# Issuing the first five loads of pass two from ScalarE's queue instead of SyncE's

## The chip, the cores and the metric

One core of a Trainium2 chip runs the whole kernel. The metric is the device time of one execution in microseconds.

## The reference

The reference scales an image of 384 x 384 pixels and 384 channels (bf16, 113 MB) by a factor for each channel, which it gets from the mean of the whole image:

```python
g = jnp.einsum("bhwc->bc", x) / (H * W)
gp = jnp.pad(g, ((0, 0), (pad, pad)))            # k = 1, so pad = 0
s = jnp.zeros_like(g)
for i in range(k):
    s = s + gp[:, i:i + C] * w1d[i]
s = _sigmoid(s)
return x * s[:, None, None, :]
```

No pixel can be scaled before the last one has been summed. So every kernel has two passes over the image, and what the on-chip memory cannot hold has to be read twice.

## The kernel before

Pass one loads all rows (a "row" is 384 channels on each of 128 partitions, 98,304 bytes in all) and sums them on TensorE. It keeps as many rows as it can in one big on-chip tile, `arena`: 71 raw, and 296 more in groups in which VectorE has folded four rows' bits into the space of three. The other 785 rows, the streamed ones, are loaded again in pass two. Pass two scales what is kept, stores it, and loads streamed rows into the places that come free.

All instructions go through a small scheduler. It takes them in program order, finds what each has to wait for from the rows that it reads and writes, and gives each transfer a semaphore of its own queue (a counter that is raised as the transfer lands, and that others can wait for):

```python
        if dma:
            q = self.queued.setdefault(eng, [])
            s.lane = (eng, len(q) % self.LANES)
            ...
            q.append(s)
    ...
                waits = [(sem(d), d.rank * (16 if d.dma else 1)) for d in s.waits]
                ...
                for h, v in waits:
                    eng.wait_ge(h, v)
                ins = s.emit()
```

An engine's queue works in order: while it waits for the semaphore of one transfer, it issues nothing behind that. (The trace before shows it. The stores that the first load of pass two needs had landed by 273.31 us. But the load stood behind a store that was issued at 274.27 us, and was itself issued at 274.70 us.) Loads and stores share one such queue, SyncE's:

```python
    def load(chunk, a, lo, hi):
        r0, n = chunk
        fl.add(
            "SP",
            lambda: nc.sync.dma_start(out=arena[:, a : a + hi - lo, :], in_=view(xf, r0, n)[:, lo:hi, :]),
            writes=rows(a, hi - lo), dma=True,
        )
    ...
    def store(chunk, a, lo, hi):
        r0, n = chunk
        return fl.add(
            "SP",
            lambda: nc.sync.dma_start(out=view(of, r0, n)[:, lo:hi, :], in_=arena[:, a : a + hi - lo, :]),
            reads=rows(a, hi - lo), dma=True,
        )
```

The order of all work of pass two is fixed when the kernel is built, by a loop that imitates the passing of time. It decides when VectorE scales rows (`scale`), when it unfolds a group, when a store is sent, and when enough places are free for the next load:

```python
        if landed and (ahead < PENDING or not can):
            chunk, a, lo, n, end = landed.popleft()
            scale(a, n)
        ...
        if got and todo < N_STREAM:
            n, a = max(got)
            n = min(n, CAP, N_STREAM - todo)
            ahead = backlog()
            if n >= BIG or n == N_STREAM - todo or (ahead < LOW and n >= 8) or ahead < LAST:
                load(STREAMED, a, todo, todo + n)
                ...
```

A load waits until the stores of the rows that it overwrites have landed. A store waits until VectorE has scaled its rows.

## Time and profile before

| | before |
|---|---|
| time, median of 6 runs | 721.47 us (720.91 to 722.41) |
| profiled span | 720.1 us |
| bytes moved | 303.8 MB, about 430 GB/s wherever the DMA is full |
| VectorE busy, whole span | 69% |
| VectorE busy, 269 to 310 us | 38.66 of 41 us |
| last load of pass one lands, first store issued | 267.5 us, 270.06 us |
| last store lands | 718.0 us |

The DMA here is the core's 16 DMA engines, which move data between the main memory and the on-chip memory. The page's slices (a digit is the busy share of a fortieth of the span, in tenths) tell when the DMA engines are full. The table by stretches gives the same for any window, with the GB/s moved. The issues and waits of SyncE's queue tell what each load and store waited for. The lines of each are in the prediction below.

### The profile page before, as it was taken

To read this page: it belongs to the slowest core of one execution; us is meant where nothing else is said; L and a number is where in the kernel's file an instruction comes from. 1 tells how busy PE (TensorE), PEld (TensorE's weight loads), DVE (VectorE), ACT (ScalarE), POOL (GpSimd) and SP (SyncE) were. 2 spreads that over 40 slices of the span, in tenths; PEclk is the share of its full clock that TensorE was granted. 3 is DMA by queue.
4 is the path that set the end of the run, shared out by engine and by line. 5 is a ranking of instruction groups with operands and counts; after the bars stand their busy time and mean duration, and the time that the engine had idled before them with its cause. 6 is when DMAs were issued, how large, how long until landed. Compare 5 with 4: busy or idle time off the path is not lost.

```text
span 720.1 us, 2041 instructions
## 1 busy us (share of the span) xinstructions
PE 213.6 (30%) x1202; PEld 0.3 (0%) x3; DVE 496.4 (69%) x470; ACT 115.4 (16%) x92; POOL 0.2 (0%) x4
## 2 busy tenths in 40 slices
PE   4678778897987770000000000000000000000000
PEld 0000000000000000000000000000000000000000
DVE  4600004788999719989899999999996991558500
ACT  3600003566777510002000000000000000000000
POOL 0000000000000000000000000000000000000000
PEclk9798999999999995555555555555555555555555
DMA  9999999999999979999999999999999999999996
GB/s 382 431 439 428 426 431 430 435 436 430 423 427 428 427 321 355 427 431 424 414 429 433 430 433 433 434 431 432 439 430 440 428 435 436 433 431 434 433 435 299
DMA packets 18877, 303.79 MB, mean 422 GB/s; under 512 B 2098, under 2 KB 2098, under 8 KB 4658
## 3 DMA queue, kind: packets, MB, share of 16 engines
q1 hardware_dynamic: 18864, 303.67, 98.7%
q8 instruction: 4, 0.07, 0.0%
q14 instruction: 7, 0.06, 0.0%
q10 hardware_dynamic: 2, 0.00, 0.0%
HBM read 190.41 MB, written 113.25 MB: 422 GB/s over the span
## 4 chain that ended last, share of the span: by engine, by line
DMA 60%; DVE 27%; PE 4%; ACT 2%; SPq 0%; issue 0%; DVEq 0%; another core or an unknown queue 0%
DMA arena<-in_x_dram 43%; DVE arena L451 19%; DMA out_dram<-arena 17%; DVE arena L275 5%; PE bank L242 4%; DVE arena L281 3%; ACT arena L312 2%; SPq L235 0%; ACT s_bf L442 0%; DVEq L112 0%; SPq L772 0%; SPq L112 0%; SPq L106 0%
## 5 line engine op out<-in xcount | busy, mean ns | idle before, releaser
L451 DVE TENSOR_TENSOR arena<-arena,s_bf 128x1536 bf16<-128x1536 bf16 (+8 forms) x103 | 242.2, 2390 | 57.8 <-DMA arena<-in_x_dram 41.9
L275 DVE TENSOR_SCALAR arena<-arena 128x1536 uint16<-128x1536 uint16 (+2 forms) x247 | 145.5, 634 | 114.9 <-DMA arena<-in_x_dram 102.2
L242 PE MATMUL bank<-arena,ones 128*128 128x384 bf16 x1151 | 205.2, 340 | 46.1 <-DMA arena<-in_x_dram 45.9
L312 ACT ACTIVATE arena<-arena 128x3072 uint16<-128x3072 uint16 (+1 forms) x38 | 102.5, 2696 | 142.4 <-DVE arena L275 142.4
L281 DVE TENSOR_TENSOR arena<-arena 128x1536 uint16<-128x1536 uint16 (+2 forms) x114 | 121.1, 1062 | 5.2 <-PE bank L242 2.7
L524 PE MATMUL bank<-odd,ones 128*128 128x1 bf16 x1 | 0.2, 184 | 329.2 <-DVE odd L519 329.2
L385 ACT COPY arena<-bank 128x512 uint32<-128x512 uint32 (+1 forms) x7 | 4.0, 571 | 61.9 <-DMA out_dram<-arena 61.8
L242 PE MATMUL bank<-zeros,ones 128*128 128x384 bf16 x48 | 8.3, 326 | 0.0
L312 ACT ACTIVATION_READ_ACCUMULATOR arena<-arena 128x1 f32 x38 | 7.1, 186 | 0.0
L385 ACT COPY bank<-arena 128x512 uint32<-128x512 uint32 (+1 forms) x7 | 3.6, 567 | 0.0
L442 ACT ACTIVATE s_bf<-bank,w_sc 128x384 bf16<-128x384 f32 x1 | 0.6, 582 | 14.5 <-PE bank L242 14.5
L255 PE MATMUL bank<-arena,ones 128*128 128x384 bf16 x1 | 0.5, 476 | 6.8 <-DMA arena<-in_x_dram 6.8
L745 ACT ACT_TABLE_LOAD x1 | 1.3, 1283 | 0.7 <-PEq L761 0.7
L342 DVE TENSOR_SCALAR w_sc<-bank 128x1 f32<-128x1 f32 x1 | 0.2, 159 | 1.1 <-PE bank L337 1.1
L332 DVE MEMSET ones<- 128x128 bf16 x1 | 0.2, 165 | 1.0 <-SPq L106 1.0
L337 PE MATMUL bank<-w_bf,ones 1*128 1x1 bf16 x1 | 0.2, 182 | 2.1 <-DMA w_bf<-in_w1d_dram 2.1
L524 PEld LDWEIGHTS bank<-odd,ones 128*128 128x128 bf16 x1 | 0.1, 103 | 588.4 <-DVE odd L519 588.4
L528 DVE CAST odd_i<-bank 128x1 int32<-128x1 f32 x1 | 0.2, 157 | 0.3 <-PE bank L524 0.3
L514 DVE TENSOR_REDUCE worst<-seen 128x1 f32<-128x38 f32 x1 | 0.2, 184 | 0.0
L519 DVE TENSOR_SCALAR odd<-worst 128x1 bf16<-128x1 f32 x1 | 0.2, 156 | 0.0
L333 DVE MEMSET zeros<- 128x64 uint32 x1 | 0.1, 112 | 0.0
L255 PEld LDWEIGHTS bank<-arena,ones 128*128 128x128 bf16 x1 | 0.1, 104 | 6.8 <-issue 6.8
(5 smaller groups left out, 0.5 us busy)
## 6 DMA issues: line engine op xcount, KB each, us to landing
arena<-in_x_dram SPq DMA_DIRECT2D x15, 4608.0 KB, 33.3
arena<-in_x_dram SPq DMA_DIRECT2D x22, 1248.0 KB, 11.3
out_dram<-arena SPq DMA_DIRECT2D x8, 3072.0 KB, 30.3
arena<-in_x_dram SPq DMA_DIRECT2D x6, 3072.0 KB, 27.4
out_dram<-arena SPq DMA_DIRECT2D x12, 1248.0 KB, 11.9
out_dram<-arena SPq DMA_DIRECT2D x3, 4608.0 KB, 39.8
arena<-in_x_dram SPq DMA_DIRECT2D x3, 4512.0 KB, 37.9
out_dram<-arena SPq DMA_DIRECT2D x3, 4512.0 KB, 27.7
```

Of the source, the lines that this page charges most:

```text
L242: return pe.add_instruction(mybir.InstMatmult(name=nc.get_next_instruction_name(), ins=[pe.lower_ap(rhs), pe.lower_ap(ones[:])], outs=[pe. ...
L255: return nc.tensor.matmul(acc, lhsT=ones[:], rhs=arena[:, i, :], start=first, stop=last)
L275: lambda: nc.vector.tensor_scalar(out=dst, in0=src, scalar1=s0, scalar2=s1, op0=op0, op1=op1),
L281: "DVE", lambda: nc.vector.tensor_tensor(out=dst, in0=a, in1=b, op=op), reads=reads, writes=writes
L312: lambda: nc.scalar.activation(out=y, in_=y, func=ACTF.Copy, accum_out=seen[:, 2 * k + i : 2 * k + i + 1]),
L332: fl.add("DVE", lambda: nc.vector.memset(ones[:], 1.0), writes=["ones"])
L337: lambda: nc.tensor.matmul(votes, lhsT=ones[0:1, :], rhs=w_bf[0:1, 0:1], start=True, stop=True),
L385: "ACT", lambda: nc.scalar.copy(dst.bitcast(u32), src.bitcast(u32)), reads=reads, writes=writes
L442: lambda: nc.scalar.activation(out=s_bf[:], in_=acc, func=ACTF.Sigmoid, scale=w_sc[:, 0:1]),
L451: lambda: nc.vector.tensor_tensor(out=v, in0=v, in1=s_bf[:, None, :].to_broadcast([P, n, C]), op=Op.mult),
L524: lambda: nc.tensor.matmul(votes, lhsT=ones[:], rhs=odd[:], start=True, stop=True),
L745: nc.scalar.preload_act_table(ACTF.Sigmoid)
```

## The change

The intent: while a load on SyncE's queue waits for a landed store, stores behind it that are ready can't be issued. So the first five loads of pass two move to the queue of ScalarE, which has nothing else to do then.

```diff
-    def load(chunk, a, lo, hi):
+    def load(chunk, a, lo, hi, queue="SP"):

         r0, n = chunk
+        start = nc.sync.dma_start if queue == "SP" else nc.scalar.dma_start
         fl.add(
-            "SP",
-            lambda: nc.sync.dma_start(out=arena[:, a : a + hi - lo, :], in_=view(xf, r0, n)[:, lo:hi, :]),
+            queue,
+            lambda: start(out=arena[:, a : a + hi - lo, :], in_=view(xf, r0, n)[:, lo:hi, :]),
             writes=rows(a, hi - lo), dma=True,
         )
...
+    n_loads, N_ASIDE = 0, 5
...
-                load(STREAMED, a, todo, todo + n)
+                load(STREAMED, a, todo, todo + n, "ACT" if n_loads < N_ASIDE else "SP")
+                n_loads += 1
```

## The prediction

> **What bounds the kernel now.** I read the page from the top. Its slices of DMA share and of moved bytes come first, because the kernel moves much more than it computes.
>
> ```profile
> span 720.1 us, 2041 instructions
> PE 213.6 (30%) x1202; PEld 0.3 (0%) x3; DVE 496.4 (69%) x470; ACT 115.4 (16%) x92; POOL 0.2 (0%) x4
> DMA  9999999999999979999999999999999999999996
> GB/s 382 431 439 428 426 431 430 435 436 430 423 427 428 427 321 355 427 431 424 414 429 433 430 433 433 434 431 432 439 430 440 428 435 436 433 431 434 433 435 299
> HBM read 190.41 MB, written 113.25 MB: 422 GB/s over the span
> ```
>
> The reader is to see that the 16 DMA engines are at nine tenths or more in 38 of 40 slices, at about 430 GB/s, while the busiest compute engine, VectorE, has 69%. 303.7 MB at 430 GB/s are 706 us; the other 14 us are the start, the gap between the passes, and the end. Pass two (scale by the sigmoid and store) begins near 269 us. The input has 113.25 MB, the same as what is written, so pass two reads again 190.41 - 113.25 = 77.2 MB and moves 77.2 + 113.2 = 190.4 MB: 443 us at 430 GB/s. Its first packets flow at 271 us and its last at 718 us, 447 us. So about 4 us in all stand between pass two and a full DMA.
>
> Where those are I asked of the table by stretches (columns: length, busy of the engines, clock, DMA share, GB/s).
>
> ```profile
> 268.00:270.00 2.00, 0.43 (x3) 0.00 (x0) 0.92 (x2) 0.58 (x1) 0.00 (x0) 1.00 0.00 0
> 270.00:272.00 2.00, 0.00 (x0) 0.00 (x0) 2.00 (x3) 0.00 (x0) 0.00 (x0) 1.00 0.56 227
> ...
> 276.00:278.00 2.00, 0.00 (x0) 0.00 (x0) 2.00 (x1) 0.00 (x0) 0.00 (x0) 0.50 0.98 270
> 278.00:280.00 2.00, 0.00 (x0) 0.00 (x0) 2.00 (x2) 0.00 (x0) 0.00 (x0) 0.50 0.91 258
> ```
>
> ```profile
> 271.00:281.00 10.00, 0.00 (x0) 0.00 (x0) 10.00 (x5) 0.00 (x0) 0.00 (x0) 0.55 0.93 332
> 281.00:345.00 64.00, 0.00 (x0) 0.00 (x0) 61.60 (x54) 4.00 (x7) 0.00 (x0) 0.50 1.01 427
> 345.00:350.00 5.00, 0.00 (x0) 0.00 (x0) 4.93 (x8) 0.00 (x0) 0.00 (x0) 0.50 1.00 392
> 350.00:718.00 368.00, 0.18 (x1) 0.10 (x1) 279.38 (x211) 0.00 (x0) 0.00 (x0) 0.50 1.00 429
> ```
>
> From 281 us on the DMA is full. The loss is 10 x (430 - 332)/430 = 2.3 us in 271 to 281, some 0.4 us in 345 to 350, and the rest at the end, where the packets thin out from 714 to 718 us because some DMA engines finish 3.6 us after others. Note 276 to 280: the engines are busy, yet move 264 GB/s. In the packet records, 6144-byte packets that elsewhere take 234 ns take 330 to 390 ns on average there, and one 2.1 us. That is slowness of packets, not lack of work.
>
> Then the queue of SyncE, which the change is about: its waits between 268 and 310 us (total us, times, longest), and its issues in order of time (start, length; each landing time named below is that of the transfer's last semaphore update in the trace).
>
> ```profile
> SPq L461 <- DVE arena L451: 37.4, 12, 14.4
> SPq L235 <- DMA out_dram<-arena: 7.8, 4, 3.0
> ```
>
> ```profile
> 270.06 4.54 SPq L461 DMA_DIRECT2D out_dram<-arena  x4
> 274.70 0.40 SPq L235 DMA_DIRECT2D arena<-in_x_dram  x1
> 275.94 10.00 SPq L461 DMA_DIRECT2D out_dram<-arena  x5
> 287.50 6.65 SPq L235 DMA_DIRECT2D arena<-in_x_dram  x3
> 294.20 0.43 SPq L461 DMA_DIRECT2D out_dram<-arena  x1
> 295.31 0.33 SPq L235 DMA_DIRECT2D arena<-in_x_dram  x1
> 301.82 9.59 SPq L461 DMA_DIRECT2D out_dram<-arena  x4
> ```
>
> The five loads concerned are the one at 274.70, the three of 287.50 to 294.15 and the one at 295.31. Stores wait almost only for VectorE (37.4 us, 12 times); loads wait for the landing of the store that frees their rows (7.8 us, 4 times, the longest 3.0).
>
> **What the Trainium skill says.** "DMA: Bandwidth & Descriptors", section "Issuing engines are not separate DMA queues": DMAs started by ScalarE and by SyncE run on the same 16 DMA engines and interleave; starting them on several engines saves only sequencer time. The trace before can't show two queues at work (its one transfer on the other queue has a few bytes), but that one queue alone holds 427 to 434 GB/s agrees that nothing is left to add. The same page, "Queues, rings and completion order": each DMA engine goes round-robin between the rings that have work, packet by packet, and the two issuing engines own one ring each. So a load on the second ring no longer stands behind the stores queued before it: it takes about half the bandwidth at once. No run so far shows this. Its "Rules for kernel authors" says that spreading DMAs over queues doesn't help bandwidth; I rest the main estimate on that.
>
> **The change part by part.** No work is added or removed: 8 + 13 + 13 + 13 + 8 = 55 rows of 98,304 bytes, 5.4 MB or 12.6 us of DMA time, change the ring. The order on VectorE and the order of stores stay. An issue takes 0.33 to 0.40 us of a sequencer; five come to 1.8 us, moved from SyncE, which here mostly waits, to ScalarE, which between the sigmoid's end (269.05) and the bank copies (330.80) does nothing.
>
> Step 1, stores that no longer wait behind a load. Issued after load 1 is the store at 275.94, which waited for VectorE anyway: 0 us. After loads 2 to 4 comes the store at 294.20; its rows were ready when VectorE ended at 293.84: 0.36 us. After load 5 comes the store at 301.82, again waiting for VectorE: 0. Sum 0.4 us of earlier issue, for a store that then lands at 306.98, 12.8 us after issue. With 12 us of work queued ahead, issuing it 0.4 us earlier ends nothing earlier: worth 0.
>
> Step 2, loads that no longer wait behind a store. Load 1 needs the first two stores, landed at 272.37 and 273.31, and stood behind the fourth store, issued at 274.27 after VectorE. It can go at about 273.35, 1.35 us sooner. Loads 2 to 5 were issued at 287.50, 290.48, 293.83 and 295.31, and the stores they need landed at 287.48, 290.46, 293.81 and 295.29: they go 0.02 us after what frees their rows, so the queue held them by nothing.
>
> Step 3, does load 1 fill the hole? From issue to first packet the first store took 0.86 us (270.06 to 270.92). Load 1's packets then begin near 274.2. The hole in the packets is 272.9 to 273.45, and the third store's packets fill from there; at 274 to 276 the DMA is already at 412 GB/s. So at most the idle parts of 277 to 280 (busy 0.93, 0.87, 0.93, together 0.27 us) are filled by 0.8 MB offered sooner. Gain 0 to 0.3 us.
>
> Step 4, sharing. Load 2 landed at 298.25, as four stores' remains were ahead. With half the bandwidth from about 288.3 its 1.28 MB (2.97 us alone) land after about 6 us, near 295. The stores it passes land later by up to the same 3 us, so loads 3 to 5 are issued 1.5 to 3 us later, yet land earlier too, near 298 to 304 instead of 301.20, 304.17 and 309.27. VectorE's one wait for a load in this stretch, 2.2 us before 309.30, goes. VectorE is then some 2 us ahead; but what it feeds is a DMA with 7 to 12 us of work queued, so the end doesn't move.
>
> Sum: 0 (step 1) - 0.15 (steps 2 and 3) + 0 (step 4): 721.45 - 0.15, about 721.2.
>
> **The rivals.** First, the hole is due to the queue's order, as the change supposes: then up to 2.3 us of 271 to 281 come back and the time is 719.2. For it speaks that the low rate begins with the first load. Against it: engines busy at 0.91 to 0.98, slow packets. A variant is that the second ring lets an engine move a store's packet while a load's is held up, which would save part of the 1.5 us of the slow packets: near 720.
>
> Second, sharing hurts: the stores passed by loads land up to 3 us later, loads that wait for those stores are issued later, and if the DMA ran dry there it would be lost: up to +3 us, 724.5. Against it: the bytes queued at any time are the same or more as long as the loads are issued, and before had a queue of 7 us at its shortest here (last load landed at 309.27, next store issued at 301.82). Alternating reads and writes packet by packet might also cost efficiency; 5% of the about 25 us in which 5.4 MB of loads and as much of stores share would be 1.3 us: 722.5.
>
> Third, VectorE were the limit: its 2.2 us of idle time would be saved, 719.2. Against it: the DMA's full slices up to 718 us.
>
> Fourth, the slow packets of 276 to 280 and 343 to 348, which leave some DMA engines up to 3.6 us behind at the end, fall otherwise: 1 to 2 us either way.
>
> **Range and chances.** The middle is 721.0, a little under the sum for the first rival, which is likelier than the second. The first and third rival bring 719, the second and fourth 723; 8 times in 10 it should lie from 718.6 to 723.2. Two per cent are 14.4 us, more than all that pass two loses to anything but moving its bytes (4 us), so faster by that is 1%; slower needs a stall that the queue of 7 us or more would have to swallow first: 1%; within, 98%.
>
> **What would show each step.** Step 1: no store of 270 to 302 issued over 0.5 us earlier for the queue's sake. Step 2: load 1 issued by ScalarE near 273.4, loads 2 to 5 within 0.1 us of a store's landing. Step 3: 271 to 281 still at 320 to 360 GB/s; near 420 there means that the first rival is right. Step 4: load 2 lands near 295, 6 to 8 us after issue instead of 10.75, the stores beside it up to 3 us later, and VectorE's wait at 309 shrinks; rate from 281 on still 425 to 430. Below 415 over 285 to 310 means that sharing costs. The prediction is wrong if the DMA shows slices below 9 tenths after 281 us, or if a rate over 436 GB/s shows that two rings carry more than one.

## More of the kernel before

The kernel before and a kernel compared with it always ran on the same chip and in the same rounds.

## The result, and the profile after

The changed kernel takes 721.87 us (median of 6 runs, 721.08 to 722.42), against 721.47 us before. The ratio is 1.0003, with a 95% interval of 0.999 to 1.0016. A ratio here is the mean time of one kernel's fast runs over that of the other's fast runs in the same rounds, so it is not quite the ratio of the medians. The time is the same.

The page of the changed kernel, its span, its DMA slices, and its queues (packets, MB, share of 16 engines):

```profile
span 719.3 us, 2044 instructions
DMA  9999999999999979999999999999999999999997
GB/s 383 426 444 431 426 428 435 436 436 427 424 426 426 428 327 349 427 432 425 422 425 437 429 439 428 430 435 430 438 423 440 429 435 435 432 432 437 430 435 320
q1 hardware_dynamic: 18144, 298.26, 96.9%
q10 hardware_dynamic: 722, 5.41, 2.0%
```

The change is in effect: 5.41 MB, the five loads, moved to queue q10. The slices look as before: 14 and 15, in which pass two begins, have 327 and 349 GB/s after 321 and 355. (The profiled span is 0.8 us shorter. The medians of all runs don't show that as a gain.)

ScalarE's issues in the changed kernel, one line for each of the five loads (start, length):

```profile
273.21 0.36 ACTq L236 DMA_DIRECT2D arena<-in_x_dram  x1
286.17 0.33 ACTq L236 DMA_DIRECT2D arena<-in_x_dram  x1
289.16 0.33 ACTq L236 DMA_DIRECT2D arena<-in_x_dram  x1
294.36 0.33 ACTq L236 DMA_DIRECT2D arena<-in_x_dram  x1
299.15 0.33 ACTq L236 DMA_DIRECT2D arena<-in_x_dram  x1
```

And what SyncE's queue waited for in the changed kernel between 268 and 310 us:

```profile
SPq L462 <- DVE arena L452: 49.0, 13, 14.4
```

The waits of loads are gone from SyncE: all that is left there is stores that wait for VectorE. That was the intent, and it worked. But the loads themselves gained little. The stores that loads 2 to 5 need landed at 286.15, 289.14, 294.34 and 299.13 us, each 0.02 us before the issue of the load. Taking a load out of the queue does not land the store that it waits for.

The stretches of pass two in the changed kernel (length, busy time of the engines, clock, DMA share, GB/s):

```profile
271.00:281.00 10.00, 0.00 (x0) 0.00 (x0) 10.00 (x5) 0.00 (x0) 0.00 (x0) 0.63 0.95 326
...
285.00:310.00 25.00, 0.00 (x0) 0.00 (x0) 22.00 (x21) 0.00 (x0) 0.00 (x0) 0.50 1.01 429
281.00:345.00 64.00, 0.00 (x0) 0.00 (x0) 59.98 (x53) 3.99 (x7) 0.00 (x0) 0.50 1.01 428
345.00:350.00 5.00, 0.00 (x0) 0.00 (x0) 4.96 (x7) 0.00 (x0) 0.00 (x0) 0.50 1.01 414
350.00:718.00 368.00, 0.19 (x1) 0.11 (x1) 280.60 (x213) 0.00 (x0) 0.00 (x0) 0.50 1.00 428
```

The slow start of 271 to 281 us is still there, at 326 GB/s after 332. In the packet records it has only moved along with the first load, from 276 to 280 us to 275 to 278.5 us. While loads and stores share the engines on two rings (285 to 310 us), the DMA moves 429 GB/s, against 426 before. In this stretch sharing costs no efficiency and brings none.

What did change is the order in which things land:

| load | issue before / after | lands before / after |
|---|---|---|
| 1 (8 rows) | 274.70 / 273.21 | 282.59 / 279.73 |
| 2 (13 rows) | 287.50 / 286.17 | 298.25 / 295.65 |
| 3 (13 rows) | 290.48 / 289.16 | 301.20 / 300.94 |
| 4 (13 rows) | 293.83 / 294.36 | 304.17 / 306.03 |
| 5 (8 rows) | 295.31 / 299.15 | 309.27 / 310.86 |

Loads 2 and 3 are issued 1.3 us earlier, but not for the queue's sake. The stores that they need start to finish no earlier than before (for load 2, the first of the 16 engines is done at 285.56 us, after 285.32 before); the engines are only less spread (0.6 us from the first to the last, after 2.2).

Loads 2 and 3 overtake stores, which then land later. The eight-row store issued at about 285.5 us, for example, lands at 299.13 us instead of 295.29. Load 5 needs that store, so it is issued 3.8 us later and lands 1.6 us later. VectorE's wait for loads between 298 and 320 us (total, times, longest), before and then after:

```profile
DVE arena L451 <- DMA arena<-in_x_dram: 2.2, 1, 2.2
```

```profile
DVE arena L452 <- DMA arena<-in_x_dram: 3.8, 2, 2.1
```

It grew by 1.6 us instead of vanishing, and the end did not move. So there are three things to test. Is it the throughput of the DMA that sets the end? How much delay does the queued work swallow? And is it sharing that made loads 4 and 5 late?

### The profile page after: what moved, and what is told of

The parts are those of the page before. It is cut to its first block, busy times and chain, and to the rows that moved or that the text cites. A ratio compares the mean times of both kernels' runs of the same rounds, so it can differ in the third digit from the quotient of the medians.

```text
span 719.3 us, 2044 instructions
## 1 busy us (share of the span) xinstructions
PE 213.0 (30%) x1202; PEld 0.3 (0%) x3; DVE 495.9 (69%) x470; ACT 115.4 (16%) x92; POOL 0.2 (0%) x4
## 3 DMA queue, kind: packets, MB, share of 16 engines
q10 hardware_dynamic: 722, 5.41, 2.0%
## 4 chain that ended last, share of the span: by engine, by line
DMA 52%; DVE 31%; ACT 5%; PE 5%; another core or an unknown queue 1%; issue 0%; SPq 0%; DVEq 0%
DMA arena<-in_x_dram 36%; DVE arena L452 20%; DMA out_dram<-arena 16%; DVE arena L276 7%; ACT arena L313 5%; PE bank L243 5%; DVE arena L282 4%; SPq L236 0%; ACT s_bf L443 0%; DVEq L112 0%; SPq L776 0%; SPq L106 0%
## 6 DMA issues: line engine op xcount, KB each, us to landing
arena<-in_x_dram SPq DMA_DIRECT2D x15, 4608.0 KB, 33.9
```

## The experiments

My theory is the prediction's: the DMA's throughput sets the end, and the queue of issued work hides what happens before it. The rivals are that the order in SyncE's queue costs time, that VectorE sets the end, and that two rings do harm because loads overtake stores.

**All loads of pass two aside.** The changed kernel with one number changed:

```diff
-    n_loads, N_ASIDE = 0, 5
+    n_loads, N_ASIDE = 0, 1000
```

> The changed kernel, but every load of pass two goes through ScalarE's queue, none through SyncE's. My theory (the DMA engines' throughput sets the end; 7 us or more are always queued): same time, 721.5 us +- 1.5, rate 425 to 434 GB/s after 281 us, though SyncE's waits for landed stores (126 us in the changed kernel) all leave its queue. Rival (order in the queue costs, but five loads were too few to show it): faster by 3 us or more. Second rival (two rings share, stores land later and loads that wait for them come later): slower by 2 us or more, with VectorE waiting longer for loads than the 4.6 us of 268 to 420 us in the changed kernel.

Measured: 727.56 us against 721.87 us, ratio 1.008 (1.0066 to 1.0094). My theory is wrong here, and the second rival holds: more of the change is slower, clearly. VectorE's waits for loads between 268 and 420 us are 8.8 us, after 4.6 in the changed kernel. The stretches where it loses:

```profile
380.00:386.00 6.00, 0.00 (x0) 0.00 (x0) 6.00 (x4) 0.00 (x0) 0.00 (x0) 0.50 1.02 336
448.00:454.00 6.00, 0.00 (x0) 0.00 (x0) 5.93 (x12) 0.00 (x0) 0.00 (x0) 0.50 1.01 369
584.00:588.00 4.00, 0.00 (x0) 0.00 (x0) 4.00 (x3) 0.00 (x0) 0.00 (x0) 0.50 0.57 209
596.00:600.00 4.00, 0.00 (x0) 0.00 (x0) 4.00 (x2) 0.00 (x0) 0.00 (x0) 0.50 0.85 301
```

The kernel before moves 434, 442, 430 and 433 GB/s in the same stretches. In the third line the DMA runs dry (share 0.57) while VectorE is busy all the time. In the first two it is busy throughout (1.02 and 1.01) and slow nevertheless. The last two runs below take this apart.

**A late load left out.** The kernel before without one load of 44 rows.

```diff
-                load(STREAMED, a, todo, todo + n)
+                if n != 44:
+                    load(STREAMED, a, todo, todo + n)
```

> The kernel before without its load of 44 rows near 608 us (wrong result on purpose: those rows keep old data). It takes 44 x 98,304 bytes = 4.33 MB out of the DMA, 10.0 us at 432 GB/s. My theory (throughput of the DMA sets the end): faster by 9 to 10.5 us, 711 to 712.5. Rival (VectorE or the order of issues sets the end): faster by under 3 us.

Measured: 711.40 us against 721.87, ratio 0.9865 (0.985 to 0.988); the result is wrong. The gain is 10.5 us by the medians and 9.7 us by the ratio, for bytes worth 10.0 us, and the DMA stays full where the load was missing:

```profile
600.00:640.00 40.00, 0.00 (x0) 0.00 (x0) 14.04 (x5) 0.00 (x0) 0.00 (x0) 0.50 1.00 430
```

Late in pass two the bytes set the end, one for one.

**VectorE delayed by three passes, and by nine.** The kernel before, with passes over the rows of the second load that leave them as they are (3 or 9 for `K`).

```diff
                 chunk, a, lo, n, end = landed.popleft()
+                if chunk == STREAMED and lo == 8:
+                    for _ in range(K):
+                        bits(flat(a, n), flat(a, n), XOR, 0, AND, 0xFFFF, rows(a, n), rows(a, n))
```

> The kernel before with three more passes of VectorE over the 13 rows of the second load of pass two, near 299 us, that change no value: about 3 x 1.5 = 4.4 us of delay for VectorE and for every store after it. My theory (the store issued at 301.82 finds 7.5 us of queued work, as the last load lands at 309.27): time unchanged within 0.7 us. Rival (VectorE or the wait of stores for it sets the end): slower by 2.2 (4.4 less its own idle 2.2) to 4.4 us.

> As the one with three, but nine passes, about 13 us of delay. My theory: the 7.5 us queued, less about 1 us from issue to first packet, are used up, and the DMA runs dry for 13 - 6.5 = 6 us: slower by 4 to 8 us, with a hole in the GB/s near 309 to 316 us and none in the run with three passes. Rival (VectorE sets the end): slower by 11 to 13 us. Rival (something other than DMA and VectorE): under 2 us.

Measured: with three, 723.56 us, ratio 1.0023 (1.0007 to 1.0038), about 1.7 us slower; with nine, 732.53 us, ratio 1.0149 (1.0134 to 1.0165), 10.7 us slower. Both are more than I expected. The nine passes come nearer to the rival's 11 to 13 us than to my 4 to 8, and the 1.7 us of the three passes lie between my 0.7 and its 2.2. The DMA with three passes (4.44 us of work), then with nine (13.42 us):

```profile
305.00:309.00 4.00, 0.00 (x0) 0.00 (x0) 4.00 (x3) 0.00 (x0) 0.00 (x0) 0.50 0.88 369
```

```profile
306.00:316.00 10.00, 0.00 (x0) 0.00 (x0) 9.83 (x7) 0.00 (x0) 0.00 (x0) 0.50 0.08 35
```

With nine, the dry stretch loses 10 x (430 - 35)/430 = 9.2 us. So the queued work swallowed 13.4 - 9.2 = 4.2 us of delay, not the 6.5 that I had worked out (7.5 less 1 from issue to first packet). I had counted to the landing of the last load, 309.27 us. But that load's first update came at 306.66 us: the DMA engines are spread over 2.6 us, and 14 of the 16 were done with it by 307.29 us. The other 1.5 us of the loss are a slow stretch after the dry one (394 GB/s in 316 to 336 us, 20 x 36/430 = 1.7 us). With three passes the DMA runs dry too, where I expected no hole: that costs 0.6 us, and a slow stretch after it (396 GB/s in 309 to 330 us) another 1.7 us.

So the theory "it is all swallowed" is right for small delays only. If VectorE is delayed early in pass two, the first 4 us or so are hidden and what goes beyond them comes through nearly in full, with some 1.5 us for a slow stretch on top.

**The five loads left out.** The kernel before, the first five loads of pass two not issued; in a second run, told below, only the first one not issued. Their outputs are wrong, which doesn't matter for the times.

```diff
+    n_loads, N_SKIP = 0, 5       # 0, 1 in the next run
...
-                load(STREAMED, a, todo, todo + n)
+                if n_loads >= N_SKIP:
+                    load(STREAMED, a, todo, todo + n)
+                n_loads += 1
```

> The kernel before without the five loads concerned (wrong result on purpose). They are 5.41 MB, 12.6 us of DMA time. My theory: not all of it is gained, because early in pass two VectorE only just feeds the DMA: the queue that lasts to 309.3 us would end at 296.7, while the next store needs VectorE until 301.8: some 5 to 6 us of hole near 297 to 303, and a gain of 5.5 to 9 us. Rival that the change rested on (stores wait behind these loads, and that costs the time): the stores go out sooner and the whole 12.6 us or more are gained. Rival that the loads are free: under 2 us.

Measured: 719.52 us against 721.22, ratio 0.9974 (0.9958 to 0.9989). Bytes worth 12.6 us are gone, and the time falls by 1.7 us. This is less than I expected, and within what I had given for the rival that these loads are free. Two stretches of the DMA, and one of the whole early part, in which the third busy number is VectorE's:

```profile
289.00:294.00 5.00, 0.00 (x0) 0.00 (x0) 5.00 (x4) 0.00 (x0) 0.00 (x0) 0.50 0.17 69
...
297.00:302.00 5.00, 0.00 (x0) 0.00 (x0) 4.97 (x5) 0.00 (x0) 0.00 (x0) 0.50 0.00 0
...
269.00:310.00 41.00, 0.00 (x0) 0.00 (x0) 40.90 (x32) 0.00 (x0) 0.00 (x0) 0.52 0.71 300
```

I had found one dry stretch and missed the other. Together they lose 9.2 us of DMA time, and a slow stretch after them (345 GB/s in 312 to 321 us) another 1.8: that is why so little of the 12.6 us is gained. VectorE is busy for 40.90 of 41 us: without the loads, it alone sets the pace there. With them (before) it is busy for 38.66 us of the same stretch. So early in pass two the DMA and VectorE are both nearly full, and each has only a few microseconds to spare against the other. For the change this means that neither half of the rival on which it rests holds: stores do not wait behind these loads (but for the 0.36 us of one), they wait for VectorE; and even loads that cost nothing would gain no more than these 1.7 us here.

**The first load left out.**

> The kernel before without the first of the five loads only (wrong result on purpose), for the hole of 276 to 280 us (264 GB/s). If the hole belongs to the first reads after the pause between the passes, whatever is read, it moves to the second load, near 289 to 293, and the gain is the load's bytes alone, 0.79 MB or 1.8 us. If it belongs to these rows or to this load's size, no hole is left and the gain is 3 to 4.5 us. If it belongs to the stores or to the moment, 276 to 280 still shows it.

Measured: 720.12 us against 721.22, ratio 0.9988 (0.9972 to 1.0003): a gain of 1.1 us by the medians that the interval does not separate from none.

```profile
276.00:280.00 4.00, 0.00 (x0) 0.00 (x0) 4.00 (x2) 0.00 (x0) 0.00 (x0) 0.50 0.93 390
288.00:292.00 4.00, 0.00 (x0) 0.00 (x0) 4.00 (x5) 0.00 (x0) 0.00 (x0) 0.50 1.01 336
```

The slow stretch moved: 276 to 280 us has 390 GB/s after 264, and 288 to 292 us, where the second load is now the first, has 336 at a full share. It belongs to the first load after the pause, whichever that is.

**The first load from other rows, and the first load's place touched beforehand.**

```diff
-                load(STREAMED, a, todo, todo + n)
+                at = N_STREAM - n if n_loads == 0 else todo      # n_loads = 0 is set above
+                load(STREAMED, a, at, at + n)
+                n_loads += 1
```

```diff
+    touched = pool.tile([P, 16], bf16, name="touched")
...
     assert summed[0] == RPP
+    fl.add(
+        "SP",
+        lambda: nc.sync.dma_start(out=touched[:], in_=view(xf, *STREAMED)[:, 0, 0:16]),
+        writes=["touched"], dma=True,
+    )
```

> The kernel before, but the first load of pass two reads the last eight of the streamed rows (read some 10 to 20 us earlier by pass one) in place of the first eight, last read near 10 us (wrong result on purpose). Same bytes, same places in the on-chip memory, same moment. If the hole of 276 to 280 us comes from where the load reads, it goes, or moves to the next load, which reads beside the first rows. If it comes from reading after writing, or from the moment, it stays and the time is the same within 0.7 us.

> The kernel before with one more tiny load at the end of pass one: 32 bytes for each of the 128 partitions, from where the first load of pass two will read; the result is right. It is served near 267 us, when the DMA is about to idle. If what makes the first load of pass two slow is that its places in memory are cold, the hole of 276 to 280 us goes and the kernel is faster by 1 to 2.5 us. If it comes from reads after writes, from the moment or from the load's size, nothing changes, within 0.7 us.

Measured: 721.30 us with other rows, wrong on purpose (ratio 1.0001, 0.9986 to 1.0017) and 721.27 us with the touch (0.9999, 0.9985 to 1.0013), both against 721.22. The same stretch in the first and in the second:

```profile
276.00:280.00 4.00, 0.00 (x0) 0.00 (x0) 4.00 (x2) 0.00 (x0) 0.00 (x0) 0.50 0.90 243
```

```profile
276.00:280.00 4.00, 0.00 (x0) 0.00 (x0) 4.00 (x2) 0.00 (x0) 0.00 (x0) 0.50 0.89 224
```

Neither where the load reads nor whether it was read just before makes the slow stretch. Together with the changed kernel, where it went with that load to the other ring, this shows that it belongs to the first load after the pause. What makes it stays open. A pattern that I only argue: the slow stretches after a dry DMA, in the two runs with a delayed VectorE and in the one without five loads (345 GB/s in 312 to 321 us), also come with the first loads that meet a short queue.

**The first load alone aside.** The changed kernel with

```diff
-    n_loads, N_ASIDE = 0, 5
+    n_loads, N_ASIDE = 0, 1
```

> The changed kernel with its first load alone on ScalarE's queue, the other four back on SyncE's. If the later landing of the fourth and fifth load (306.0 and 310.9 us in the changed kernel, 304.2 and 309.3 before) comes from sharing, they land here as before, within 0.5 us, and VectorE waits for loads near 309 us once for about 2.2 us rather than twice. Time as before within 0.7 us in any case.

Measured: 722.28 us against 721.66, ratio 1.0009 (0.9992 to 1.0026), the same. Loads 4 and 5 land at 302.71 and 307.36 us. That is earlier than in both other kernels, and by more than the 0.5 us that I allowed: the spread of the DMA engines is smaller than before here (0.7 us at load 5, after 2.6). VectorE's wait between 298 and 320 us:

```profile
DVE arena L452 <- DMA arena<-in_x_dram: 0.6, 1, 0.6
```

With 2.2, 3.8 and 0.6 us of this wait, the three kernels take the same time. So the lateness of loads 4 and 5 does come from loads 2 to 5 sharing with the stores, and it is swallowed.

**The first 15 loads aside, and all but the first 15.** The changed kernel with the first of these two edits, and with both:

```diff
-    n_loads, N_ASIDE = 0, 5
+    n_loads, N_ASIDE = 0, 15
```

```diff
-                load(STREAMED, a, todo, todo + n, "ACT" if n_loads < N_ASIDE else "SP")
+                load(STREAMED, a, todo, todo + n, "SP" if n_loads < N_ASIDE else "ACT")
```

> The changed kernel with the first 15 loads of pass two aside, those up to about 380 us in the run with all aside. If the loss of that run (727.6 against 721.9 us) is made where it shows holes, the one at 380 to 386 us comes back (336 GB/s there; 6 x (430 - 336)/430 = 1.3 us), those at 448 to 454, 584 to 588 and 596 to 600 don't: slower by 1 to 2 us. If each load aside costs the same, 15 of some 30 give about 2.8 us. If the early loads cost nothing, 0.

> The reverse: the first 15 loads of pass two go through SyncE as before, all later ones through ScalarE. By the holes of the run with all aside: slower by 3 to 4.5 us, with the DMA running dry near 584 to 588 us and slow stretches near 448 and 597. If what cost the time in that run was the sharing early in pass two: within 1 us.

Measured, against 721.66 us: 724.22 us with the first 15 (ratio 1.003, 1.001 to 1.0051), and 728.10 us with the later ones (1.0083, 1.0066 to 1.01), 6.4 us more, where I expected 3 to 4.5. The first run has the slow stretch of 380 to 386 us again (361 GB/s) and not the later ones. It is 0.5 us slower than the range I gave, and about what an equal cost for every load would give too. But the second run shows that the cost is not equal. (The two costs don't add up to that of all loads aside either: 2.6 and 6.4 against 5.7 us. That stays open.) ScalarE's own work does not explain the loss: its copies near 330 us, which now stand in one queue with loads, start at 330.65 us with 15 loads aside and at 330.52 us with all aside, after 330.80 before.

In the second run the DMA runs dry, and VectorE does not wait:

```profile
586.00:592.00 6.00, 0.00 (x0) 0.00 (x0) 6.00 (x4) 0.00 (x0) 0.00 (x0) 0.50 0.36 109
```

It waited before that. VectorE's one wait for a landed store between 500 and 620 us, in the kernel before and in the one with the late loads aside:

```profile
DVE arena L275 <- DMA out_dram<-arena: 6.2, 1, 6.2
```

```profile
DVE arena L276 <- DMA out_dram<-arena: 22.7, 1, 22.7
```

VectorE needs the places of rows whose store has landed before it can unfold the next group. Before, that store (32 rows) lands at 548.29 us. With the late loads aside it lands at 573.26 us. Of these 25 us, 8.5 were lost earlier: the store is issued at 522.84 us instead of 514.36, as VectorE had by then waited longer for loads (16.9 us between 268 and 500 us, after 8.3 in the kernel before). The other 16.5 us are added in flight, 50.4 us after 33.9: the loads of 47 and 48 rows, which had landed after this store, now overtake it on their own ring. VectorE starts again 25 us later, its next stores come later by as much, and the queue is empty before they do. So one way in which sharing costs is shown: transfers that something waits for are overtaken.

It is not the only one. In the run with the first 15 loads aside, 380 to 386 us are slow at a full share (1.06), so that the DMA does not run dry there. In the packet records loads are 97% or more of the bytes from 382 to 386 us, so hardly any store shares the engines then. It looks like the slow stretch at 276 to 280 us; what makes it stays open.

No experiment points to a version that beats both kernels: with 1, 5, 15 or all loads aside, or the later ones alone, the time was the same or slower.

## Why the prediction was right

**The sum** was right: about 721.2 us, with 721.0 as the middle, against 721.87. (721.45 - 0.15 is 721.3; the text has 721.2.) The change moves no bytes away, and of its five transfers the queue held only the first, for 1.4 us. That part was no luck. That the end did not move although the queued work was shorter than I thought was partly luck, as told below.

**Step 1**, stores that no longer wait: right. The store that I named is issued at 293.84 us instead of 294.20; nothing else moved for the queue's sake.

**Step 2**, loads that no longer wait: right. Load 1 goes at 273.21 us (I said 273.35); the other four follow a landed store by 0.02 us.

**Step 3**, the hole: right. It is not filled, 326 GB/s after 332. But load 1's packets began at 275.40 us and not near 274.2: on the second ring it took 2.2 us from issue to first packet, not the 0.86 that I took over from a store. The first rival is refuted: the hole follows the first load from queue to queue, and when that load is left out it goes to the next.

**Step 4**, sharing: right in kind, wrong in several sizes. "With half the bandwidth from about 288.3" failed: load 2's first packet came at 289.68 us, 3.5 us after its issue, and all that the engines moved in between were packets that SyncE had issued before. (Three stores were still under way when load 2 was issued in the kernel before, not the four that I counted.) It landed 9.5 us after issue instead of 6 to 8. "Loads 3 to 5 are issued 1.5 to 3 us later" failed too: load 3 went 1.3 us earlier, load 4 0.5 later and load 5 3.8 later. And that they "land earlier too, near 298 to 304" failed for loads 4 and 5, which landed 1.9 and 1.6 us later than before: I had let each load gain from sharing without following the store that the next one waits for. VectorE's wait did not go, but grew.

**"With 7 to 12 us of work queued"** was the term that was mis-sized: the run with nine passes shows that the work queued at 301.8 us swallows 4.2 us. The conclusion stood because the change delays VectorE by only 1.6 us. With a delay of 4.4 us it would have failed, as the run with three passes shows (1.7 us slower). That the change stays below this was luck: the prediction had VectorE 2 us ahead, not behind.

**The second rival**, that sharing hurts, I gave too little: five loads are too few for it, but with all loads aside it costs 5.7 us. Of the two ways I gave it, a DMA that runs dry is seen in the runs with all and with the late loads aside. Alternating cost nothing in 285 to 310 us (429 GB/s). The slow stretch of the run with 15 aside is neither. **The third rival**, that VectorE is the limit, is half right: not for the end, but early in pass two it has just 2.3 us in 41 to spare. **The fourth rival**, slow packets that fall otherwise, moved the rate in 345 to 350 us (414 GB/s after 392) and the spread of the DMA engines at the last store (2.7 us after 3.7), and no more than the noise of the time.

## What to carry to other kernels

Before moving a transfer to another queue, look at what ended its wait: if it is issued 0.02 us after the landing of what it needs, the queue held nothing, and another queue gives it nothing. A second ring is not free either: its transfers overtake those already queued, and if an engine waits for one of the overtaken, the delay comes back larger (here a store that took 16.5 us longer, in a run that took 6.4 us more). And measure how much delay the queued work really swallows by delaying something on purpose; the landing time of the slowest DMA engine made it look like 7.5 us, where 4.2 were swallowed.

## What the Trainium skill lacked or had wrong

- "DMA: Bandwidth & Descriptors", "Queues, rings and completion order", says that each DMA engine goes round-robin between rings, packet by packet. The trace agrees once both rings flow: from 289.7 us on, packets of 9,984 bytes of the two queues alternate on an engine, mostly one by one. (The records don't name the engine; they fall into 16 chains in which a packet starts as the last one ends.) What the section lacks is how long a ring waits for its first turn: a load issued at 286.17 us onto an idle ring had its first packet at 289.68 us, while the other ring was full; with the other ring nearly empty it took 2.2 us (273.21 to 275.40).
- The same page's "Issuing engines are not separate DMA queues" and its "Rules for kernel authors" say that spreading over queues doesn't help bandwidth and only saves issue time. The rate agrees (429 GB/s on two rings, 426 on one). That it can cost time, in part through stores that are overtaken, is not there: 727.56 against 721.87 us with all loads aside, 728.10 against 721.66 with the later ones.
- No page that I read has the slow stretch at the first load after the pause in loads: 224 to 298 GB/s for 4 us at a DMA share of 0.89 to 0.97, on either queue, wherever it reads. Its cause stays open.
